# Making the router's gates once for all tiles, and scaling the first expert's results by them

## The chip, the cores and the metric

One core of one Trainium2 chip runs the whole program. The metric is the device time of one execution in microseconds (us); a kernel's time is the median over its runs.

## What is computed

Sliding-window attention gives x (2304 tokens by 512), a mixture of experts with one expert a token turns it into a new x, and a dense layer follows. All is fp32. Cut to what matters here:

```python
logits = xn @ en.T / tau                  # xn, en: rows over their norm
expert_idx = np.argmax(logits, axis=1)
probs = np.exp(logits - logits.max(-1, keepdims=True))
probs /= probs.sum(-1, keepdims=True) + 1e-09
gate_w = probs[np.arange(N), expert_idx]
for e in range(E):                        # E = 8, D = 512, F = 1024
    mask = expert_idx == e
    h = np.maximum(x[mask] @ w1[e], 0.0)
    out[mask] = gate_w[mask, None] * (h @ w2[e])
```

A gate is positive, so it can be multiplied into a token's row ahead of the expert or into the expert's result.

## The kernel before

**Numbers.** TensorE's products take each fp32 operand as a high and a low part (hh and hl, xh and xl, wh and wl) and sum three matmuls. The high part is made by ScalarE (ACT, L87), the low one by VectorE (DVE) or GpSimd (POOL) in L88.

**Attention.** 36 steps, written out as a list; PE's and SyncE's (SP) queues are in the order of the program, those of DVE, ACT and POOL are set by a scheduler. A step makes scores (spb, L241), masked maxima on DVE (L249), exponentials on ACT (pe, L259 and L262), their transposes (pt, L268, copied as pT by ACT in L270), and products with v (po, L280), which DVE scales into xs (L289). Tokens come in 18 tiles of 128. A finished tile is written to x_dram and turned (tpx, L375).

**The router** hangs on the steps. `later(n + d, ...)` puts a piece of it behind a later step, and the table ROUTED gives the distances for the tile groups 0 to 3, 4 to 8, 9 to 12 and 13 to 15; tiles 16 and 17 follow behind the attention. For each group `route_rank` finds the expert of a token as a one-hot row oh (L402 to L410), `route_count` and `route_list` its place in that expert's list, and `part(..., 0, 2)` with `listed` puts the token numbers into the lists: DVE makes Qv (L441), PE sums Qv and lhot into rt (`rt<-Qv,lhot`). Then the gates: `route_norm` (POOL, L450), `route_gate` (twelve small DVE operations and one Exp on ACT, L457 to L473) and `part(..., 2, 5)` with `listed` for the gates' three bf16 parts.

**The first expert.** Behind tile 12 `route_first` chooses the expert with the longest list (efi, L486), and SP loads its weights; ACT makes wh. Its first NA = 208 rows are computed inside the attention's end: `first_rows` gathers them (L108, by POOL's indirect DMAs from the token numbers io), `first_turn` makes their gates go (L492, L493), multiplies the rows (`gated`, L112), transposes them on PE (L119) and splits them into xh and xl. `first_part` is their hidden layer (L132) and second product (pa, L126), evacuated to ya and written to y0_dram.

**Behind the attention** its other 256 rows are gathered in three pieces, the gates of tiles 13 to 17 are made, `route_order` sorts the experts, `route_tokens` gives all lists (idx), and the three pieces are multiplied by their gates and turned. `route_gates` gives all gates by expert (gsl). Then `expert(n)` runs for the eight experts. While one runs, `fetch` gathers the rows of the next and multiplies them by gsl (L112). The buffers of gathered rows, and of expert 0's pieces, are five (pool m3, tag xg); those of `hidden` in PSUM are four (pool p1):

```python
m3 = pool(mc, "m3", 5, side="right", reuse_waits="tile")
p1 = pool(mc, "p1", 4, space=PSUM, reuse_waits="tile")
```

The dense layer follows.

Of the kernel before, what the change touches and what calls it, by code (L numbers as in the profile page):

```python
# [20 lines left out]
def tile_kernel(ctx, tc, q, k, v, emb, tau, w1, w2, w_in, w_out, s_in, b_in, out, x_dram, y_dram, y0_dram, wi_dram, wo_dram):  # L21
# [414 lines left out]

    def part(t0, t1, j0, j1):
        w, ts_ = j1 - j0, slice(t0, t1)
        vb_ = [128, t1 - t0, w, E * KT]
        Qv = rp2.tile(vb_, BF16, tag=f"Qv{w}", name="Qv")  # L440
        made.append(nc.vector.tensor_tensor(Qv, Q[:, ts_].rearrange("p t e k -> p t (e k)").unsqueeze(2).to_broadcast(vb_),  # L441
                                val[:, ts_, j0:j1].unsqueeze(3).to_broadcast(vb_), op=ALU.mult).ins)
        return Qv
# [212 lines left out]
    def fin(slots, pT):  # L656
# [36 lines left out]
        later(n + d[4], lambda: listed(t0, t1, 0, 2, q[0]))  # L693
        if t1 == TL:
            return
        later(n + d[5], lambda: route_norm(t0, t1))
        later(n + d[6], lambda: route_gate(t0, t1), BEHIND)
        later(n + d[7], lambda: q.append(part(t0, t1, 2, 5)), BEHIND)
        later(n + d[8], lambda: listed(t0, t1, 2, 5, q[1]))
        if t1 == TF:  # L700
            later(n + d[9], first_turn)
            later(n + d[4], first_rows)
# [19 lines left out]
    def first_turn():  # L722
        go = first_gates(0, 2)
        for j, r, xg in xga:
            gated(xg, go[:r, j:j + 1])
            turn(ps3, xg, xa, j * 128)
# [26 lines left out]


    def first_part():

        w, ht = sets[0], []
        yield from hidden(ps3, "tp", w, xa, NA, ht, la, NA)
        ya = raw_p.tile([128, 1024], F32, tag="raw", name="ya")[:, :ND * NA].rearrange("p (c n) -> p c n", c=ND)
        for d in range(ND):  # L760
            ps = ps1.tile([128, NA], F32, tag="pt" if d % 2 else "po", name="pa")
            for f in range(NF):
                three(ps, w2part(w, f, d), ht[f], f == 0, f == NF - 1)
            evac(ya, d, ps)
            if d == ND - 1:
                nc.scalar.dma_start(y0cols[:, :, :NA], ya)
            yield
# [3 lines left out]

    ROUTED = {3: ((0, 4), (4, 5, 6, 7, 9, 10, 11, 12, 14)),
# [154 lines left out]
    with tc.manual_schedule(engines={mybir.EngineType.PE}):  # L927
# [8 lines left out]
        for t, xt in xts:  # L936
            route_logits(t, xt)
        route_norm(TF, NTT)
        route_rank(TL, NTT)
# [13 lines left out]
        for j, c0, r, o in ((0, NA - 128, 128, 0), (1, 0, 128, 256 - NA), (2, 0, CAPS[0] - 384, 384 - NA)):  # L953
            xg = m3.tile([128, DM], F32, tag="xg", name="xg")[:r]
            gather(xg, x_dram, io[:r, j:j + 1])
            parts.append((xg, j, c0, r, o))
        route_gate(TF, NTT)
        order = route_order()
        route_tokens(order[1])
        qv = part(TF, NTT, 2, 5)  # L960
        some(7)
        listed(TF, NTT, 2, 5, qv)
        go = first_gates(1, 4)
        some(8)
        for xg, j, c0, r, o in parts:
            gated(xg, go[:r, j:j + 1])
            if j == 2:
                for _ in part_:
                    pass
            turn(ps3, xg, x0, o, c0)  # L970
        route_gates(order[1])
        for _ in part_:
            pass
    xts = {0: x0}

# [9 lines left out]
    def expert(n, w, xt, mid):  # L985
# [10 lines left out]
        for d in range(ND):  # L996
            evac(y, d, ps[d])
        if n == 0:
            nc.scalar.dma_start(y0cols[:, :, NA:NA + N], y)
            nc.scalar.dma_start(ycols[:, :, NA:NA + N], y)  # L1000
# [118 lines left out]
    x2 = []  # L1119
    OV = 4  # L1120
    RR = 1
    for n in range(E):
# [16 lines left out]
        def mid(i):  # L1139
            if n == 0 and i == 0:  # L1140
                begin()
            if last and i == OV:
                fs.close()
# [154 lines left out]
```

## Time and profile before

| | |
|---|---|
| median of 3 runs | 831.58 us (831.35 to 832.79) |
| profiled execution, its own time | 830.12 us |
| its span | 828.4 us |
| mean granted clock of TensorE, as a share of full speed | 0.974 |

The profile is of one execution. Its timelines give each instruction its start and duration in us, with the engine's idle time before it and what ended that in brackets; runs of equal instructions share a row (x4), and matmuls of a row overlap, so that the next row's start tells more than a row's duration. Busy times by stretch end with the granted clock of TensorE (PEclk, 1.00 is 2.4 GHz, 0.50 is 1.2 GHz), the DMA engines' busy share and GB/s. A line number is that of the kernel before.

### The profile page before, as it was taken

How to read it: one execution, taken by the hardware profiler on the slowest of the kernel's cores; microseconds unless marked ns; L12 is line 12 of the kernel's file. 1: busy time of each engine (PE TensorE's matmuls, PEld its weight loads, DVE VectorE, ACT ScalarE, POOL GpSimd, SP SyncE). 2: the span in 40 equal slices, each digit the busy share in tenths (PEclk: the TensorE clock that was granted, in tenths of full speed). 3: DMA queues.
4: the chain of work that ended last, by engine and by line, in shares of the span. 5: the costliest groups of instructions: out<-in, count | busy, mean ns of one | idle time of the engine just before them, and what ended most of it. 6: DMA issues, size and time to landing. Idle time of an engine off the chain costs nothing.

```text
span 828.4 us, 16563 instructions
## 1 busy us (share of the span) xinstructions
PE 783.8 (95%) x6350; PEld 718.3 (87%) x6350; DVE 505.3 (61%) x1310; ACT 394.0 (48%) x796; POOL 195.5 (24%) x184
## 2 busy tenths in 40 slices
PE   6988887889999999899899999999999999999996
PEld 4776676789999999899889999999998999999985
DVE  3766676856778758689575555666646444444442
ACT  6886867415335536445454444444435333332231
POOL 3422335032014244335002222222200110101010
PEclk9997997999999999899999999999999999999999
DMA  9965837156759868775652333333314111100000
GB/s 197 209 182 147 209 97 239 51 185 218 210 178 302 256 223 266 248 244 216 213 186 99 104 102 102 127 127 107 114 63 128 51 52 37 41 26 26 27 26 26
DMA packets 100642, 117.16 MB, mean 141 GB/s; under 512 B 38884, under 2 KB 72164, under 8 KB 100560
## 3 DMA queue, kind: packets, MB, share of 16 engines
q1 hardware_dynamic: 91072, 99.11, 39.7%
q0 software_dynamic: 3232, 10.24, 3.5%
q10 hardware_dynamic: 6256, 6.72, 2.4%
q8 instruction: 51, 0.84, 0.4%
q14 instruction: 31, 0.25, 0.1%
HBM read 91.52 MB, written 24.53 MB: 140 GB/s over the span
## 4 chain that ended last, share of the span: by engine, by line
PE 47%; DMA 2%; issue 1%; DVE 0%; ACT 0%; SPq 0%; POOLq 0%; ACTq 0%
PE p L126 47%; DMA raw<-wi_dram 1%; DMA raw<-wo_dram 1%; DMA y_dram<-y 0%; DMA out_dram<-o,ids 0%; ACT wh L87 0%; DVE wl L88 0%; SPq L96 0%; POOLq L1293 0%; DVE y L747 0%; DVE o L1243 0%; SPq L1112 0%; ACT r L1205 0%; SPq L1039 0%; ACTq L1006 0%
## 5 line engine op out<-in xcount | busy, mean ns | idle before, releaser
L126 PE MATMUL p<-xh,wh 128*128 128x256 f32 x576 | 162.3, 282 | 1.1 <-ACT r L1205 1.1
L126 PE MATMUL p<-xl,wh 128*128 128x256 f32 x576 | 162.4, 282 | 0.0
L126 PE MATMUL p<-xh,wl 128*128 128x256 f32 x576 | 161.7, 281 | 0.0
L1205 ACT ACTIVATE r<-p 128x256 f32<-128x256 f32 x144 | 55.3, 384 | 166.5 <-PE p L126 161.8
L1206 DVE SCALAR_TENSOR_TENSOR r<-r,s_bc 128x256 f32<-128x256 f32 x144 | 79.9, 557 | 77.1 <-ACT r L1205 76.9
L126 PE MATMUL p<-wh,gh 128*128 128x512 f32 x288 | 113.0, 392 | 0.0
L126 PE MATMUL p<-wl,gh 128*128 128x512 f32 x288 | 113.0, 392 | 0.0
L126 PE MATMUL p<-wh,gl 128*128 128x512 f32 x288 | 113.0, 392 | 0.0
L88 DVE TENSOR_TENSOR wl<-raw,wh 128x1024 fp32r<-128x1024 f32 x76 | 107.7, 1424 | 8.2 <-ACT wh L87 8.1
L126 PEld LDWEIGHTS p<-xh,wh 128*128 128x128 f32 x576 | 108.7, 189 | 2.0 <-ACT r L1205 1.3
L126 PEld LDWEIGHTS p<-xl,wh 128*128 128x128 f32 x576 | 108.6, 188 | 0.8
L126 PEld LDWEIGHTS p<-xh,wl 128*128 128x128 f32 x576 | 109.0, 189 | 0.0
L1029 POOL TENSOR_TENSOR fl<-fl,fs 128x512 f32<-128x512 f32 x32 | 45.8, 1433 | 251.2 <-DVE fs L1028 219.2
L87 ACT ACTIVATE wh<-raw 128x1024 fp32r<-128x1024 f32 x80 | 83.3, 1055 | 9.1 <-DMA raw<-in_moe_w_dram 3.9
L126 PE MATMUL p<-hh,wh 128*128 128x256 f32 (+5 forms) x256 | 78.7, 307 | 0.0
L126 PE MATMUL p<-hl,wh 128*128 128x256 f32 (+5 forms) x256 | 76.9, 301 | 0.0
L126 PE MATMUL p<-hh,wl 128*128 128x256 f32 (+5 forms) x256 | 76.9, 300 | 0.0
L1212 ACT ACTIVATE gh<-r,b_bc 128x256 fp32r<-128x256 f32 x144 | 72.5, 503 | 7.7 <-DVE r L1206 7.5
L1213 DVE SCALAR_TENSOR_TENSOR gl<-r,b_bc,gh 128x256 fp32r<-128x256 f32 x144 | 71.2, 494 | 3.1 <-ACT gh L1212 3.1
L1244 POOL DMA_INDIRECT out_dram<-o,ids x18 | 18.6, 1036 | 203.8 <-DVE o L1243 182.8
L126 PEld LDWEIGHTS p<-wh,gl 128*128 128x128 f32 x288 | 54.1, 188 | 12.2
L126 PEld LDWEIGHTS p<-wh,gh 128*128 128x128 f32 x288 | 54.1, 188 | 11.4
(222 smaller groups left out, 1463.9 us busy)
## 6 DMA issues: line engine op xcount, KB each, us to landing
raw<-in_moe_w_dram SPq DMA_DIRECT2D x64, 512.0 KB, 4.9
raw<-y_dram SPq DMA_DIRECT2D x18, 512.0 KB, 3.8
vb<-in_v_dram SPq DMA_DIRECT2D x64, 128.0 KB, 3.7
fr<-in_moe_w_in_dram SPq DMA_DIRECT2D x16, 512.0 KB, 5.2
fr<-in_moe_w_out_dram SPq DMA_DIRECT2D x16, 512.0 KB, 4.0
k<-in_k_dram SPq DMA_DIRECT2D x32, 144.0 KB, 3.3
q<-in_q_dram SPq DMA_DIRECT2D x32, 144.0 KB, 3.3
x_dram<-xs SPq DMA_DIRECT2D x8, 512.0 KB, 3.2
```

Source lines behind the costliest of these rows:

```text
L87: a = nc.scalar.activation(hi, src, AF.Copy)
L88: return a.ins, le.tensor_tensor(lo, src, hi.bitcast(F32), op=ALU.subtract).ins
L126: nc.tensor.matmul(ps, a[x], b[y], start=first and j == 0, stop=last and j == 2)
L1029: nc.gpsimd.tensor_tensor(lf, lf, sg.bitcast(F32), op=ALU.mult)
L1205: nc.scalar.activation(r, ps, AF.Relu)
L1206: nc.vector.scalar_tensor_tensor(r, r, s_bc, r, op0=ALU.mult, op1=ALU.mult)
L1212: nc.scalar.activation(gh, r, AF.Identity, bias=b_bc)
L1213: nc.vector.scalar_tensor_tensor(gl, r, b_bc, gh.bitcast(F32), op0=ALU.add, op1=ALU.subtract)
L1244: nc.gpsimd.indirect_dma_start(out=out, out_offset=bass.IndirectOffsetOnAxis(ap=ids[:, k:k + 1], axis=0), in_=o, in_offset=None)
```

## The change

The gates leave the attention's steps: `route_norm`, `route_gate`, `part(..., 2, 5)` and its `listed` no longer stand in ROUTED. The first expert's rows, the 208 of `first_part` and the 256 others, are turned as they were gathered. The gates of all 18 tiles are made at one place behind the attention: one `route_norm`, one `route_gate` on 18 columns, two Qv of nine tiles each in buffers of m3, and 18 `listed` matmuls together, ahead of expert 0's hidden layer. The first expert's gates go are copied along 128 columns (gob); `first_scale`, behind the second tile of expert 0's hidden layer, turns them by four matmuls (gp) into a row that stands on every partition (grow), and DVE multiplies ya and later expert 0's y by it ahead of their DMAs. `tc.issue_after` keeps the scheduler from putting `route_order`, `route_tokens` and the gates ahead of the last Qv of the token numbers.

```diff
--- before.py
+++ after.py
@@ -434,10 +434,14 @@
         nc.vector.tensor_tensor(Q[:, ts_], oh[:, ts_].unsqueeze(3).to_broadcast([128, n, E, KT]),
                                 kj.unsqueeze(2).to_broadcast([128, n, E, KT]), op=ALU.mult)

-    def part(t0, t1, j0, j1):
+    def part(t0, t1, j0, j1, tp=None):
         w, ts_ = j1 - j0, slice(t0, t1)
         vb_ = [128, t1 - t0, w, E * KT]
-        Qv = rp2.tile(vb_, BF16, tag=f"Qv{w}", name="Qv")
+        n_ = (t1 - t0) * w * E * KT
+        if tp:
+            Qv = tp.tile([128, 1024], BF16, tag="xg", name="Qv")[:, :n_].rearrange("p (t w k) -> p t w k", w=w, k=E * KT)
+        else:
+            Qv = rp2.tile(vb_, BF16, tag=f"Qv{w}", name="Qv")
         made.append(nc.vector.tensor_tensor(Qv, Q[:, ts_].rearrange("p t e k -> p t (e k)").unsqueeze(2).to_broadcast(vb_),
                                 val[:, ts_, j0:j1].unsqueeze(3).to_broadcast(vb_), op=ALU.mult).ins)
         return Qv
@@ -691,14 +695,8 @@
         later(n + d[2], lambda: route_list(t0, t1))
         later(n + d[3], lambda: q.append(part(t0, t1, 0, 2)))
         later(n + d[4], lambda: listed(t0, t1, 0, 2, q[0]))
-        if t1 == TL:
-            return
-        later(n + d[5], lambda: route_norm(t0, t1))
-        later(n + d[6], lambda: route_gate(t0, t1), BEHIND)
-        later(n + d[7], lambda: q.append(part(t0, t1, 2, 5)), BEHIND)
-        later(n + d[8], lambda: listed(t0, t1, 2, 5, q[1]))
         if t1 == TF:
-            later(n + d[9], first_turn)
+            later(n + d[5], first_turn)
             later(n + d[4], first_rows)

     def first_weights():
@@ -720,9 +718,7 @@
             xga.append((j, r, xg))

     def first_turn():
-        go = first_gates(0, 2)
         for j, r, xg in xga:
-            gated(xg, go[:r, j:j + 1])
             turn(ps3, xg, xa, j * 128)

     highs, lows = [], []
@@ -752,26 +748,41 @@
     y0cols = y0_dram.rearrange("(c p) n -> p c n", p=128)


+    early = []
+
+    def first_scale(gob):
+
+        gp = p1.tile([128, KT, 128], F32, tag="tp", name="gp")
+        for j in range(KT):
+            nc.tensor.matmul(gp[:, j], gob[:, j], ident, start=True, stop=True)
+        grow = m1.tile([128, KT * 128], F32, name="grow")
+        nc.scalar.activation(grow, gp.rearrange("p j n -> p (j n)"), AF.Copy)
+        scaled(early[0], grow, 0, NA)
+        nc.scalar.dma_start(y0cols[:, :, :NA], early[0])
+        early.append(grow)
+
+    def scaled(y, grow, c0, n):
+        nc.vector.tensor_tensor(y, y, grow[:, c0:c0 + n].unsqueeze(1).to_broadcast([128, ND, n]), op=ALU.mult)
+
     def first_part():

         w, ht = sets[0], []
         yield from hidden(ps3, "tp", w, xa, NA, ht, la, NA)
         ya = raw_p.tile([128, 1024], F32, tag="raw", name="ya")[:, :ND * NA].rearrange("p (c n) -> p c n", c=ND)
+        early.append(ya)
         for d in range(ND):
             ps = ps1.tile([128, NA], F32, tag="pt" if d % 2 else "po", name="pa")
             for f in range(NF):
                 three(ps, w2part(w, f, d), ht[f], f == 0, f == NF - 1)
             evac(ya, d, ps)
-            if d == ND - 1:
-                nc.scalar.dma_start(y0cols[:, :, :NA], ya)
             yield

     now = [0]
     TOACT = (("k", 0), ("k", 1), ("q", 0))

-    ROUTED = {3: ((0, 4), (4, 5, 6, 7, 9, 10, 11, 12, 14)),
-              4: ((4, 9), (3, 4, 5, 6, 7, 8, 9, 10, 12)),
-              12: ((9, 13), (2, 3, 3, 3, 4, 4, 4, 4, 6, 7)),
+    ROUTED = {3: ((0, 4), (4, 5, 6, 7, 9)),
+              4: ((4, 9), (3, 4, 5, 6, 8)),
+              12: ((9, 13), (2, 3, 3, 3, 4, 6)),
               15: ((13, 16), (2, 3, 3, 3, 4))}
     LATE = 11
     xa = []
@@ -935,7 +946,7 @@
         some(4)
         for t, xt in xts:
             route_logits(t, xt)
-        route_norm(TF, NTT)
+        route_norm(0, NTT)
         route_rank(TL, NTT)
         some(5)
         route_count(TL, NTT)
@@ -954,23 +965,27 @@
             xg = m3.tile([128, DM], F32, tag="xg", name="xg")[:r]
             gather(xg, x_dram, io[:r, j:j + 1])
             parts.append((xg, j, c0, r, o))
-        route_gate(TF, NTT)
-        order = route_order()
-        route_tokens(order[1])
-        qv = part(TF, NTT, 2, 5)
+        with tc.issue_after(made[-1]):
+            order = route_order()
+            route_tokens(order[1])
         some(7)
-        listed(TF, NTT, 2, 5, qv)
-        go = first_gates(1, 4)
         some(8)
         for xg, j, c0, r, o in parts:
-            gated(xg, go[:r, j:j + 1])
             if j == 2:
                 for _ in part_:
                     pass
             turn(ps3, xg, x0, o, c0)
-        route_gates(order[1])
         for _ in part_:
             pass
+        with tc.issue_after(made[-1]):
+            route_gate(0, NTT)
+            qvs = [part(t, t + NTT // 2, 2, 5, tp=m3) for t in (0, NTT // 2)]
+        for t, qv in zip((0, NTT // 2), qvs):
+            listed(t, t + NTT // 2, 2, 5, qv)
+        go = first_gates(0, KT)
+        gob = m3.tile([128, KT, 128], F32, tag="xg", name="gob")
+        nc.vector.tensor_copy(gob, go.unsqueeze(2).to_broadcast([128, KT, 128]))
+        route_gates(order[1])
     xts = {0: x0}

     al.close()
@@ -996,6 +1011,7 @@
         for d in range(ND):
             evac(y, d, ps[d])
         if n == 0:
+            scaled(y, early[1], NA, N)
             nc.scalar.dma_start(y0cols[:, :, NA:NA + N], y)
             nc.scalar.dma_start(ycols[:, :, NA:NA + N], y)
             return
@@ -1118,6 +1134,7 @@
     rest = route_rest(*order)
     x2 = []
     OV = 4
+    GR = 2
     RR = 1
     for n in range(E):
         last = n == E - 1
@@ -1139,6 +1156,8 @@
         def mid(i):
             if n == 0 and i == 0:
                 begin()
+            if n == 0 and i == GR:
+                first_scale(gob)
             if last and i == OV:
                 fs.close()
                 with tc.tile_pool(name="mo", bufs=4) as mo:
```

On DVE, in the router's piece for tiles 9 to 12 inside the attention (L402 to L410 find the expert, L283 to L289 scale a step's result), what goes:

```order
-L461 TENSOR_TENSOR L<-logit,nrm 128x32
 L406 TENSOR_TENSOR eq<-logit,mxs 128x32
 L283 TENSOR_SCALAR rc<-po 128x4
 L408 TENSOR_TENSOR eq<-eq,w_202 128x32
-L463 TENSOR_TENSOR mxs<-mxs,nrm 128x4
 L284 RECIPROCAL rc<-rc 128x4
 L409 TENSOR_REDUCE km<-eq 128x4
-L464 TENSOR_TENSOR L<-L,mxs 128x32
 L289 TENSOR_TENSOR xs<-po,rc 128x2x2x64
 L410 TENSOR_TENSOR oh<-w_202,km 128x32
-L467 TENSOR_REDUCE gt<-L 128x4
```

Three operations of the gates stood between logit and oh and are gone; so are L467 and those behind it.

On PE, the end of expert 0's preparation before (pa is the first part's second product, the xg of 80 columns the last piece of expert 0's rows, tp of 256 columns its hidden layer):

```order
L126 MATMUL pa<-hl,wh 128x208
L126 MATMUL pa<-hh,wl 128x208
L119 MATMUL tp<-ident,xg 128x80 [waits DVE_49]
L119 MATMUL tp<-ident,xg 128x80 x3
L132 MATMUL tp<-xh,wh 128x256 [waits DVE_49,Activation_49]
L132 MATMUL tp<-xh,wh 128x256 x3
L132 MATMUL tp<-xh,wl 128x256 x4
```

The same place in the changed kernel, where this pair of rows for lhot stands 18 times before the hidden layer follows:

```order
L126 MATMUL pa<-hl,wh 128x208
L126 MATMUL pa<-hh,wl 128x208
L119 MATMUL tp<-ident,xg 128x80 [waits DMASW4_49]
L119 MATMUL tp<-ident,xg 128x80 x3
L316 LDWEIGHTS lhot
L316 MATMUL rt<-Qv,lhot 128x96
```

The transposes now wait for the gather's DMA and not for DVE, and the 18 listed matmuls stand where hidden followed at once.

On DVE, the start of expert 0 before (xl are the splits of expert 0's rows, gsl scales the rows of expert 1, hl belongs to expert 0's hidden layer):

```order
L549 TENSOR_REDUCE gsl<-pr 128x32
L112 TENSOR_SCALAR xg<-xg,gsl 128x512
L88 TENSOR_TENSOR xl<-tp,xh 128x4x48
L88 TENSOR_TENSOR xl<-tp,xh 128x4x128
L747 COPY ya<-pa 128x208
L112 TENSOR_SCALAR xg<-xg,gsl 128x512
L88 TENSOR_TENSOR xl<-tp,xh 128x4x80
L112 TENSOR_SCALAR xg<-xg,gsl 128x512
L112 TENSOR_SCALAR xg<-xg,gsl 16x512
L737 SCALAR_TENSOR_TENSOR hl<-tp,hh 128x256
L112 TENSOR_SCALAR xg<-xg,gsl 128x512
```

In the changed kernel, with its own line numbers, behind the splits xl:

```order
L987 COPY gob<-go_3063 128x512
L553 TENSOR_REDUCE gsl<-pr 128x32
L733 SCALAR_TENSOR_TENSOR hl<-tp,hh 128x256
L112 TENSOR_SCALAR xg<-xg,gsl 128x512
L733 SCALAR_TENSOR_TENSOR hl<-tp,hh 128x256
L112 TENSOR_SCALAR xg<-xg,gsl 128x512
L88 TENSOR_TENSOR wl<-raw,wh 128x1024
L733 SCALAR_TENSOR_TENSOR hl<-tp,hh 128x256
L112 TENSOR_SCALAR xg<-xg,gsl 128x512
L88 TENSOR_TENSOR wl<-raw,wh 128x1024
L112 TENSOR_SCALAR xg<-xg,gsl 16x512
L765 TENSOR_TENSOR ya<-ya,grow 128x832
```

The products with gsl stood ahead of the splits and the first hl, and now stand between the hl; gob stands ahead of the first hl and the scaling of ya ahead of the fourth.

## Rows read from the trace of the kernel before

**Rows 1.** Page, part 1: engine, busy us (share of the span), instructions.
```profile
PE 783.8 (95%) x6350; PEld 718.3 (87%) x6350; DVE 505.3 (61%) x1310; ACT 394.0 (48%) x796; POOL 195.5 (24%) x184
```

**Rows 2.** Busy time by stretch: length, engines' busy us, PEclk, DMA share, GB/s.
```profile
118.00:147.20 29.20, 23.92 (x400) 19.53 (x399) 19.83 (x116) 21.80 (x51) 13.90 (x9) 0.82 0.57 192
...
178.80:194.30 15.50, 13.34 (x103) 13.21 (x102) 11.21 (x22) 6.94 (x12) 0.97 (x1) 0.89 0.65 205
```

**Rows 3.** The same view, finer: the three stretches of low granted clock.
```profile
130.40:139.60 9.20, 8.17 (x104) 6.78 (x105) 4.19 (x24) 6.43 (x11) 8.21 (x5) 0.50 0.94 343
...
160.70:164.00 3.30, 3.30 (x19) 3.30 (x17) 3.30 (x11) 0.34 (x1) 0.00 (x0) 0.52 0.00 0
...
181.40:184.80 3.40, 3.40 (x16) 3.40 (x17) 2.36 (x7) 0.38 (x1) 0.00 (x0) 0.52 0.58 195
```

**Rows 4.** Timeline of PE, end of attention: start, us, operation, [idle before, releaser].
```profile
124.16 0.55 PE L375 MATMUL tpx<-ident,xs 128*128 128x128 f32 x3 [0.67 <-DVE xs L289]
...
126.33 0.66 PE L268 MATMUL pt<-ident,pe 128*128 128x128 f32 x4 [0.28 <-ACT pT L270]
127.68 0.66 PE L268 MATMUL pt<-ident,pe 128*128 128x128 f32 x4 [0.69 <-ACT pT L270]
...
130.40 1.03 PE L316 MATMUL rt<-enT,xt 128*64 128x8 f32 x16 [1.47 <-DVE pr L499]
...
143.67 0.95 PE L119 MATMUL tp<-ident,xg 128*128 128x128 f32 x8 [0.69 <-DVE xg L112]
```

**Rows 5.** Timeline of DVE, end of attention.
```profile
120.62 0.17 DVE L457 TENSOR_SCALAR nrm<-nrm 128x4 f32<-128x4 f32 x1 [0.93 <-POOL nrm L450]
...
122.12 0.99 DVE L461 TENSOR_TENSOR L<-logit,nrm 128x32 f32<-128x32 f32 x1
...
127.20 0.13 DVE L486 CAST efi<-ff 1x1 int32<-1x1 f32 x1
...
141.70 1.20 DVE L492 TENSOR_TENSOR go<-li 128x2 f32<-128x2 f32 x1
...
143.13 0.88 DVE L112 TENSOR_SCALAR xg<-xg,go 128x512 f32<-128x512 f32 x2
```

**Rows 6.** Timeline of ACT, end of attention.
```profile
135.73 1.06 ACT L87 ACTIVATE wh<-raw 128x1024 fp32r<-128x1024 f32 x1 [1.28 <-DMA raw<-in_moe_w_dram]
...
144.57 0.40 ACT L262 ACTIVATE pe<-sm,mn 128x128 f32<-128x128 f32 x1 [1.34 <-DVE mn L249]
```

**Rows 7.** Timeline of PE, from the first part to expert 0.
```profile
159.65 0.17 PE L316 MATMUL rt<-oh,tri 128*128 128x16 bf16 x1 [1.90 <-DVE oh L410]
...
172.28 0.39 PE L316 MATMUL rt<-Qv,lhot 128*128 128x96 bf16 x5
172.49 0.34 PE L126 MATMUL pa<-hh,wh 128*128 128x208 f32 x1
...
178.78 0.44 PE L119 MATMUL tp<-ident,xg 80*128 80x80 f32 x4
181.38 1.19 PE L132 MATMUL tp<-xh,wh 128*128 128x256 f32 x4 [2.16 <-DVE xl L88]
...
184.84 0.63 PE L132 MATMUL tp<-xh,wl 128*128 128x256 f32 x4
...
194.26 0.28 PE L126 MATMUL p<-hh,wh 128*128 128x256 f32 x1
```

**Rows 8.** Timeline of DVE, start of expert 0.
```profile
177.13 0.48 DVE L112 TENSOR_SCALAR xg<-xg,go 80x512 f32<-80x512 f32 x1 [1.98 <-DMA xg<-x_dram,io]
...
180.49 0.49 DVE L112 TENSOR_SCALAR xg<-xg,gsl 128x512 f32<-128x512 f32 x1 [2.55 <-DMA xg<-x_dram,idx]
...
188.83 1.22 DVE L88 TENSOR_TENSOR wl<-raw,wh 128x1024 fp32r<-128x1024 f32 x1
```

**Rows 9.** Timeline of POOL.
```profile
154.44 1.20 POOL L450 TENSOR_TENSOR nrm<-ss,half 128x5 f32<-128x5 f32 x1 [11.56 <-DVE ss L380]
```

**Rows 10.** Tile xg from 130 to 215: its gathers, issue to landing.
```profile
DMA to landing us min/median/max: 3.2/5.8/8.5
```

## Prediction

> **What bounds the kernel now.** I read the page's busy shares first, then the busy time by stretch, then the timelines of the stretches that lose something. TensorE (PE) is busy 783.80 of 828.4 us, VectorE (DVE) 505.3 [rows 1]: all that does not fill PE is free as long as PE does not wait for it. By stretch, the losses that this change can reach lie in the end of the attention, 118.00 to 147.20, where PE is busy 23.92 of 29.20 us, and around the start of expert 0, 178.80 to 194.30, with 13.34 of 15.50 [rows 2]. The reader should also see there that busy is not the same as fast: in three stretches the granted clock is 0.50 to 0.52, so the lower of the two levels, 1.2 GHz [rows 3].
>
> The PE timeline of the first place shows the waits: 0.67 for xs of DVE, 0.28 and 0.69 for ACT, 1.47 for DVE's pr, 0.69 for a gathered row tile that DVE multiplies by its gates [rows 4]. Of the second place it shows the last transposes of expert 0's rows at 178.78, a wait of 2.16 us for DVE's xl, hidden from 181.38, and four groups of matmuls at the low clock [rows 7].
>
> **The change, part by part.** The sum is made against the profiled execution, 830.12 us; the median of the runs is 831.58, so 1.46 more, and I add that at the end.
>
> *Attention's end.* Twelve small gate operations a tile group, a Qv of three parts, a pow on POOL and the product of the first rows with their gates leave DVE. Of those that lie ahead of PE's waits, three weigh: DVE waits 0.93 us for POOL's nrm, L461 takes 0.99, go and the product of two tiles 1.20 and 0.88 [rows 5]; with some eight ops of 0.1 us from start to start between them DVE runs up to 2.7 us ahead before the first rows. All five waits of PE [rows 4], 3.80 us together, then lose their cause. What is late next: efi, the number of the first expert, is read at 127.20 [rows 5], and that expert's weights are loaded behind it. ACT rounds them in queue order, waits 1.28 us for one to land, and attention's pe stands behind it; later ACT idles 1.34 us for DVE's mn [rows 6], which go and the products hold up. efi can come 0.67 (xs) plus some 0.9 us of gate operations earlier, 1.6; the wait of 0.69 for the gathered tile and 0.3 of ACT's 1.34 go behind that. Gain 1.6 + 1.0 = 2.6. Bounds: 0, if the weights' landing moves nothing, and 3.8, all the waits. I take 2.6, since the rows name the next releaser. The transposes of the first rows now stand ahead of the last but one step's po and wait for the gather itself; these gathers are issued as much earlier as their list, so I cost that at nothing; if the cover goes, it is case C.
>
> *The wait of 1.90 us for oh* at 159.65 [rows 7]: interleaved gate ops leave DVE. Their successive starts are 0.1 us apart and three stand between logit and oh: 0.3 (0 to 0.4). The low clock behind it [rows 3] I leave as it is.
>
> *Start of expert 0.* Before, from the start of the last transposes to hidden it takes 181.38 - 178.78 = 2.60 us; DVE waits 2.55 us for a gather of expert 1 [rows 8], and the split into xl, which ends PE's wait [rows 7], stands behind that in its queue. After, that product stands behind hidden's first hl, and PE has 18 listed matmuls instead of a pause. Five of them take 0.21 from start to the next start (172.28 to 172.49) [rows 7], so 0.042 each and 0.75 for 18. 0.44 of transposes and 0.75 make 1.2 to 1.25: gain 1.35. Five matmuls leave the block ahead of it: 0.21.
>
> *The clock there.* The first four groups of hidden take 184.84 - 181.38 = 3.46 us, the next 20 take 194.26 - 184.84 = 9.42, 0.47 each [rows 7]. So the low clock [rows 3] costs 3.46 - 1.88 = 1.58. It fell behind the pause of 2.16; without that pause I take it as returned: 1.58 (0 to 1.58).
>
> *What is added.* Four fp32 matmuls gp of 128x128: eight transposes of that size take 0.95 [rows 4], so 0.5. The new copy gob (a pass over 512 elements, 0.4 to 0.6 by the products of 0.88 for two and by the split of 1024 in 1.22 [rows 5, 8]) precedes the first hl on DVE; the scaling of ya passes 832 elements, by the 1.22 of 1024 about 1.0; the last scaling 1.22 lies behind expert 0, in DVE's slack. Hidden's tiles have four buffers, a tile takes 3 x 0.47 = 1.41, so DVE may fall behind by about three of them before PE waits. Expert 1's gathers now wait for PE to free their buffers, and DVE has their products ahead of the later hl. I take 0.4 for all of it; bounds 0 and 2.3, the latter worked out under D.
>
> *The gate chain at the end.* One pow of 18 columns (1.20 for 5 columns [rows 9]: between 1.2 if it is flat and 4.3 if it grows with the columns) ends before DVE needs it, since POOL has nothing else there. Twelve operations of 0.2 to 0.3 on DVE replace as many for 5 tiles; they delay io, the list of expert 0's remaining rows, by 0.65 at most. The last of these rows have landed at 177.13 [rows 8], 1.65 ahead of their transposes at 178.78 [rows 7]: 1.0 stays in hand. The two Qv of 864 elements, by the 1.22 of 1024 again about 1.0 each [rows 8], lie behind io. Cost 0, with case E if that cover is gone.
>
> Sum: -2.6 - 0.3 - 1.35 - 0.21 - 1.58 + 0.5 + 0.4 = -5.1. 830.1 - 5.1 = 825.0; with 1.46, **826.4**.
>
> **The rivals.**
> *B, the clock does not come back.* Hidden's first groups stay slow as they were: 826.4 + 1.6 = 828.0. For it: a low clock also stands in 130.40 to 139.60 [rows 3], where PE is busy most of the time. Against it: the low clock at 181.38 begins right at the pause that goes. The Trainium skill ("TensorE: Matmul & The Clock Gate", section "Why this matters for your kernels") lays a drop in the middle of a kernel to pauses longer than any of these. By that rule the pause of 2.16 us is not the cause and B would hold; the rows show the low clock directly behind pauses of 1.47, 1.90 and 2.16, so they speak against it, and B gets 0.15.
> *C, the attention gives nothing.* If weights, ACT or the first rows' gathers only swap places with the old waits, 2.6 us are lost: 829.0. For it: ACT's wait of 1.28 for a weight [rows 6], and the first rows' transposes, which now stand ahead of po, spb and pt in PE's queue, nearer to their gather. Chance 0.12.
> *E, the gate chain is late.* Single small operations sometimes take about a microsecond (L461 0.99, go 1.20, [rows 5]) where others of their kind take 0.2. Two of those among twelve dependent ones delay io by 0.65 + 1.8; with 1.0 in hand PE waits 1.4 in front of the transposes; a pause of 1.47 has been followed by the low clock [rows 3, 4], 1.6, and up to 1.35 of the transition may go as well: 829.4 to 830.8, say 830.3. Chance 0.12.
> *D, slower: expert 1's gathers block DVE.* Counted from the start of the last transposes, T: the four gathers start behind one another at 1.25 us distance once PE frees the buffers, the fourth at about T + 3.0. With the longest landing seen, 8.5 [rows 10], it is there at T + 11.5, and its product, ya's scaling and hl (together 1.9) end at T + 13.4. PE wants that hl's buffer for its eighth tile at T + 1.25 + 7 x 1.41 + 0.5 = T + 11.6: a wait of 1.8, with the earlier gathers up to 2.3. That alone, with a low clock of 1.6 behind it, is 829.9. Every further microsecond of landing is one of PE: slower than 833.2 from landings of about 12.3, at 13 us 833.9. For it: the gathers share the DMA engines with expert 1's weights. Against: the median landing is 5.8 [rows 10], and then nothing waits. Chance 0.08.
>
> **How the numbers follow.** A, the forecast, 0.53, by itself 823.5 to 828; B 0.15, C 0.12, E 0.12, D 0.08. Down to 823.0 reach the full 3.8 (1.2 more), an uncovered 0.4, and up to 1.8 if the low clock at 130.40 goes too. Up to 830.8 lie B, C and most of E; what is left out is D, the end of E and a little below. A measurement of this kernel can tell about 0.2%, 1.7 us: faster is below 829.9, slower above 833.2. Faster: A, B and most of C, 0.78; same: E and the rest of C, 0.14; slower: D, 0.08.
>
> **What would show it.** In the changed profile PE's waits between 118 and 147 should sum to under 1.5 us and hidden of the first part start at about 144.7; 18 listed matmuls should stand between transposes and hidden with no wait over 0.5, and hidden's first groups take 0.47, not 0.87. B shows as slow groups behind a closed gap, C as waits at the first rows' transposes or at pe, E as a wait at expert 0's transposes or at listed, D as waits of hidden's later groups for hl with DVE idle for an xg gather. If PE's gain behind 194.30 or ahead of 118 is over 0.5 us either way, I have missed a cause there.

## The result, and the profile after

The change takes 821.98 us (median of 6 runs, 817.35 to 825.65), the kernel before beside it 831.47 us (828.41 to 832.84): a ratio of 0.9885, 95% interval 0.9844 to 0.9925. Forecast were 826.4 us and 823.0 to 830.8: the sign was right, the size too small. The profiled execution took 824.65 us (span 822.9 us, mean clock 0.978). Medians below are of all runs of a kernel, while the ratios leave out slow ones, which only `gates_later` has (840.59 and 841.39 of twelve).

Page of the change, part 1, for [rows 1]: PE is busy 3.0 us less, with 8 matmuls more.

```profile
PE 780.8 (95%) x6358; PEld 716.8 (87%) x6358; DVE 500.8 (61%) x1263; ACT 393.1 (48%) x794; POOL 192.9 (23%) x181
```

One pair of traces misleads here, since executions of one kernel differ. I traced both kernels three times and cut PE's timelines at the same instructions; the table has means of three, and in the last column the first traces of both, all in us. The mark "oh of tiles 9 to 12" lies near 124 before, behind the wait of 0.67 for xs [rows 4], so that this part of the forecast for the attention's end stands in that row.

| PE, from one mark to the next | before | change | difference | forecast | first pair |
|---|---|---|---|---|---|
| start to oh of tiles 0 to 3 | 60.83 | 61.55 | +0.7 | 0 | +1.7 |
| to tpx near 79 | 18.87 | 15.94 | -2.9 | 0 | -3.7 |
| to oh of tiles 4 to 8 | 20.91 | 21.53 | +0.6 | 0 | +1.0 |
| to oh of tiles 9 to 12 | 23.14 | 20.66 | -2.5 | -0.67 | -3.8 |
| to hidden of the first part | 22.71 | 22.60 | -0.1 | -1.93 | +2.1 |
| to its pa | 20.31 | 20.18 | -0.1 | -0.3 | +1.7 |
| to expert 0's hidden | 15.36 | 12.95 | -2.4 | -1.56 | -1.9 |
| to its second product | 12.46 | 12.26 | -0.2 | -0.68 | -0.6 |
| to expert 1's hidden | 13.23 | 13.23 | 0 | 0 | 0 |
| expert 1 | 37.75 | 37.01 | -0.7 | 0 | -0.9 |
| experts 2 to 4 | 90.12 | 90.62 | +0.5 | 0 | +0.5 |
| expert 5 to the dense layer | 93.50 | 93.31 | -0.2 | 0 | -0.2 |
| dense layer | 392.15 | 390.78 | -1.4 | 0 | -1.4 |
| sum | 821.3 | 812.6 | -8.7 | -5.1 | -5.4 |

The first pair came out at the forecast sum (824.65 against 825.0), by other terms: that is luck. The two rows of expert 0 up to its second product count together, since before's third trace has its pause ahead of the transposes and not behind them (last section): 27.8 before and 25.2 after, or 27.4 without that trace, so -2.2 where -2.24 was forecast. The +0.7 at the start is a low clock near 46 to 53 that is longer in two of the change's traces; three kernels edited far from there (`go_shared`, `y_late`, `pause_filled`) show it too, so it is not laid to the change. The three readings that matter:

**Ahead of 118, and up to oh of tiles 9 to 12.** Busy time by stretch, before and then the third trace of the change (columns as in [rows 2]): the clock is back.

```profile
60.00:84.00 24.00, 19.41 (x242) 15.23 (x239) 15.52 (x87) 17.49 (x40) 6.25 (x6) 0.79 0.58 153
84.00:118.00 34.00, 29.21 (x500) 23.62 (x500) 24.30 (x136) 25.01 (x56) 10.61 (x10) 0.95 0.68 171
```

```profile
60.00:84.00 24.00, 18.53 (x302) 14.55 (x302) 15.48 (x83) 19.48 (x46) 7.18 (x7) 1.00 0.68 186
84.00:118.00 34.00, 31.32 (x585) 25.43 (x584) 24.65 (x143) 26.76 (x58) 10.85 (x10) 1.00 0.65 161
```

PE's wait there, and DVE ahead of it, in the timelines of the kernel before:

```profile
69.08 1.14 PE L280 MATMUL po<-vb,pT 128*64 128x65 f32 x16 [2.35 <-DVE xs L289]
```

```profile
66.39 0.96 DVE L441 TENSOR_TENSOR Qv<-Q,val 128x256 bf16<-128x256 bf16 x2
67.38 0.16 DVE L283 TENSOR_SCALAR rc<-po 128x4 f32<-128x4 f32 x1
...
68.30 0.17 DVE L284 RECIPROCAL rc<-rc 128x4 f32<-128x4 f32 x1
68.50 0.42 DVE L289 TENSOR_TENSOR xs<-po,rc 128x256 f32<-128x256 f32 x1
```

and in the third trace of the change:

```profile
68.90 0.69 PE L280 MATMUL po<-vb,pT 128*64 128x65 f32 x16 [1.50 <-DVE xs L289]
```

```profile
67.09 0.47 DVE L445 TENSOR_TENSOR Qv<-Q,val 128x256 bf16<-128x256 bf16 x1
67.59 0.16 DVE L283 TENSOR_SCALAR rc<-po 128x4 f32<-128x4 f32 x1
67.79 0.18 DVE L284 RECIPROCAL rc<-rc 128x4 f32<-128x4 f32 x1
...
68.34 0.42 DVE L289 TENSOR_TENSOR xs<-po,rc 128x256 f32<-128x256 f32 x1
```

Before, two Qv and four masked maxima (between the two rc) stand ahead of xs; the scheduler of the changed program puts one Qv and two maxima there. A row gives the shape of its first instruction, so it hides that the second Qv is the gates' own, of three parts. The groups of before's DVE by shape, 55 to 125, have it:

```profile
L441 DVE TENSOR_TENSOR Qv<-Q,val 128x384 bf16<-128x384 bf16 x1 | 0.5, 544 | 0.0
```

From the first Qv to xs it takes 2.11 us before and 1.25 after; 0.49 of the difference goes with the gates' Qv, 0.37 with the two maxima. The wait falls from 2.35 to 1.50 us, and the 16 matmuls behind it take 0.69 and not 1.14: no low clock follows. In all eleven traces with these gates in the steps the wait is 2.35 or 2.36 and the clock of 60 to 84 is 0.79; in all seven without, 1.50 and 0.86 to 1.00. The gain is the clock and not the wait: over the whole stage to tpx PE stands idle 4.1 us before and 4.3, 3.9 and 4.3 after, and is busy 14.6 to 14.9 before and 10.9, 13.4 and 10.9 after.

**118 to 147.** PE of the change, first trace, for [rows 4]:

```profile
122.67 0.66 PE L268 MATMUL pt<-ident,pe 128*128 128x128 f32 x4 [0.88 <-ACT pT L270]
...
124.23 0.64 PE L316 MATMUL rt<-enT,xt 128*64 128x8 f32 x16 [0.28 <-DVE pr L503]
...
129.70 0.69 PE L280 MATMUL po<-vb,pT 128*64 128x65 f32 x16 [1.03 <-DVE xs L289]
...
132.34 1.12 PE L268 MATMUL pt<-ident,pe 128*128 128x128 f32 x4 [1.36 <-ACT pT L270]
...
137.08 0.79 PE L119 MATMUL tp<-ident,xg 80*128 80x80 f32 x4 [1.06 <-ACT xt L377]
...
144.52 1.16 PE L132 MATMUL tp<-xh,wh 128*128 128x208 f32 x4
```

ACT there, for [rows 6]:

```profile
126.25 1.06 ACT L87 ACTIVATE wh<-raw 128x1024 fp32r<-128x1024 f32 x1 [1.81 <-DMA raw<-in_moe_w_dram]
...
130.17 1.06 ACT L87 ACTIVATE wh<-raw 128x1024 fp32r<-128x1024 f32 x1 [1.31 <-DMA raw<-in_moe_w_dram]
```

Of the old waits that for pr is down from 1.47 to 0.28, and those for the gathered tile and the first xs are gone. New ones stand at ACT's pT and xt, 0.88, 1.36 and 1.06, and ACT itself idles for weights, as it did before [rows 6]. The 1.03 for an xs is old: it stood before too, at 136.59, and [rows 4] lacks it. So PE's waits from 118 to 148 sum to 4.9 us, where the forecast had under 1.5 as its sign and before had 5.2. Hidden starts at 144.52, near the forecast 144.7, but because the stages ahead are shorter: luck again.

**Start of expert 0.** PE of the change, first trace, for [rows 7]:

```profile
177.42 0.44 PE L119 MATMUL tp<-ident,xg 80*128 80x80 f32 x4
177.70 0.93 PE L316 MATMUL rt<-Qv,lhot 128*128 128x96 bf16 x18
178.45 0.72 PE L132 MATMUL tp<-xh,wh 128*128 128x256 f32 x4
179.01 0.64 PE L132 MATMUL tp<-xh,wl 128*128 128x256 f32 x4
...
182.77 1.05 PE L757 MATMUL gp<-ident,gob 128*128 128x128 f32 x8
183.58 0.72 PE L132 MATMUL tp<-xh,wh 128*128 128x256 f32 x4
...
190.71 0.28 PE L126 MATMUL p<-hh,wh 128*128 128x256 f32 x1
```

The 18 listed matmuls take 0.75 (177.70 to 178.45), no pause is left, and hidden runs at full clock from its first group (granted clock 1.00 in 178 to 194).

### The profile page after: what moved, and what is told of

Same layout as the page of the kernel before. It is cut to its first block, busy times and chain, and to the rows that moved or that the text cites. A ratio compares the mean times of both kernels' runs of the same rounds, so it can differ in the third digit from the quotient of the medians.

```text
span 822.9 us, 16533 instructions
## 1 busy us (share of the span) xinstructions
PE 780.8 (95%) x6358; PEld 716.8 (87%) x6358; DVE 500.8 (61%) x1263; ACT 393.1 (48%) x794; POOL 192.9 (23%) x181
## 4 chain that ended last, share of the span: by engine, by line
PE 50%; issue 0%; DMA 0%; POOLq 0%; DVE 0%
PE p L126 50%; PE tp L132 1%; DMA out_dram<-o,ids 0%; POOLq L1312 0%; DVE o L1262 0%; POOLq L1263 0%
## 5 line engine op out<-in xcount | busy, mean ns | idle before, releaser
L126 PEld LDWEIGHTS p<-wl,gh 128*128 128x128 f32 x288 | 54.1, 188 | 11.3
```

Of the source, the lines that this page charges most:

```text
L126: nc.tensor.matmul(ps, a[x], b[y], start=first and j == 0, stop=last and j == 2)
```

## The experiments

My theory after the result: the attention ahead of 118 gains by a shorter pause and the clock behind it; expert 0's start gains as forecast; the dense layer gains by where its tiles lie. The rival: executions differ, and one pair of traces shows chance. Ratios below are to the kernel before, run beside each kernel on its chip, with 95% intervals.

### Both kernels again

No edit.

> The kernel before once more, for a second trace. Theory 1: ratio 1.000 within 0.002, and the low-clock stretches of the attention lie elsewhere than in the first trace (20.4 us lost up to 420), while the one behind the pause ahead of expert 0's hidden layer (181 to 185) stands again, since its pause does. Rival (low clock is placed by the program): the same stretches within a microsecond or two.

> The changed kernel once more, for a second trace and more times. Theory 1 (the stretches of low clock move between executions, and every one costs what its length says): the ratio to the kernel before stays near 0.9885, so about 822, and the second trace loses another sum to low clock than the first (16.8 us up to 420) while the stage of hidden of expert 0 still takes full clock from its first group. Rival (the first profile was the typical one and the other runs chance): ratio near 0.993, about 825.

> The kernel before, for a third trace. In three kernels made from it, on one chip, DVE stood for 4.6 us ahead of the copy of ya and the last transposes came 4.4 us later; the two traces of before, on other chips, have no such stop. If it comes from the code of the kernels that were edited, it is absent here; if from the chip, it may stand here or not. The dense layer takes 392.15, expert 1 38.0.

> The changed kernel a third time, for the comparison with the next run on the same chip. Theory: ratio 0.989 to 0.992 to the kernel before; in its trace 390.8 for the dense layer, 37.0 for expert 1, 1.0 to 1.7 from the last transposes to hidden of expert 0, no low clock behind it.

Before: 831.69 us, 0.9991 [0.9965, 1.0017]; its third trace is of one run, 829.67. The change: 825.06, 0.9911 [0.9879, 0.9943], and 819.89, 0.9855 [0.9819, 0.9892]: the first lies between its theory and its rival, the second below what was expected. The expectation that before's low clock would lie elsewhere failed: stretches from 48.2, 68.6, 130.1 and 181.3 stood at 47.8, 68.2, 129.7 and 180.9 the second time, so most of them belong to the program. The stages in which the change is shorter in every trace are that to tpx (15.25, 17.35 and 15.22 against 18.68 to 18.98), that to oh of tiles 9 to 12 (20.66, 20.67, 20.66), expert 0's and the dense layer. From oh of tiles 9 to 12 to hidden the change took 24.83, 21.58 and 21.40: the first trace had a low clock from 131 to 149, the others a shorter one. There the rival holds: that one trace shows chance.

### Gates back in the attention

`gates_early` is the change with the gates of tiles 0 to 12 in the steps again:

```diff
-    ROUTED = {3: ((0, 4), (4, 5, 6, 7, 9)),
+    ROUTED = {3: ((0, 4), (4, 5, 6, 7, 9, 10, 11, 12, 14)),
...
-        route_norm(0, NTT)
+        route_norm(TF, NTT)
...
-            route_gate(0, NTT)
+            route_gate(TF, NTT)
```

> The change with the gates of tiles 0 to 12 left in the attention's steps as before; all else of the change stays (rows not multiplied, results scaled, start of expert 0). Theory 1 (about half of the gain comes from the gate operations leaving the attention, the rest from expert 0's start): 826 to 828. Rival (the gain is nearly all in the rows that are no longer multiplied and in expert 0's start): 821 to 824, as fast as the change. Second rival (it is nearly all in the gates): 829 to 832.

> The change with the gates of tiles 0 to 12 left in the attention, a second time and beside the change. The first pair of traces has the start of the first part, less the time lost to low clock ahead of it, at 132.4 to 132.9 in the change and at 133.6 to 135.8 in the kernels with gates in the attention, so 2.2 us. Theory (this is the attention's share of the gain): this run 2 to 3 us slower than after_third, and 135 again in the trace. Rival (it is scatter of the low clock): the same within 1 us.

825.98 us, 0.9925 [0.9897, 0.9953], and 824.23, 0.9896 [0.9863, 0.993]. Beside the change on the same chip its mean lies 2.1 above (826.6 to 824.5) and 4.7 above (824.4 to 819.7). In both traces the stage to tpx is 18.8 again and that to oh of tiles 9 to 12 is 22.8, hidden of the first part starts at 147.60 and 149.59. So some 2 to 5 us of the gain are the gates' leaving the steps, and the rest is expert 0 and what follows.

`gates03_early` puts back the gates of tiles 0 to 3 alone, far ahead of the place that I had costed:

```diff
+        if t0 == 0:
+            later(n + d[5], lambda: route_norm(t0, t1))
+            later(n + d[6], lambda: route_gate(t0, t1), BEHIND)
+            later(n + d[7], lambda: q.append(part(t0, t1, 2, 5)), BEHIND)
+            later(n + d[8], lambda: listed(t0, t1, 2, 5, q[1]))
```

> The change with the gates of tiles 0 to 3 alone left in the attention at their old distances (10, 11, 12, 14 steps); the other fourteen tiles' gates are made at the end. Theory (these twelve operations hold up xs near 69 us, the pause of 2.35 in place of 1.50 lowers the clock from 68 to 80, 5.1 us): the trace shows PEclk near 0.79 from 60 to 84 and the time is 3 to 5 us above the change, 825 to 827. Rival (the low clock at 68 comes with some executions, whatever stands there): 821 to 823 as the change, and a full clock there.

826.27 us, 0.9903 [0.9871, 0.9934]. Its PE timeline, DVE timeline and busy time by stretch:

```profile
70.48 1.14 PE L280 MATMUL po<-vb,pT 128*64 128x65 f32 x16 [2.35 <-DVE xs L289]
```

```profile
67.79 0.96 DVE L445 TENSOR_TENSOR Qv<-Q,val 128x256 bf16<-128x256 bf16 x2
```

```profile
60.00:84.00 24.00, 19.45 (x257) 15.37 (x256) 16.82 (x93) 16.66 (x37) 6.31 (x7) 0.79 0.57 149
```

The two Qv, the 2.35 and the 0.79 are back, the stage to tpx is 18.73 and that to oh of tiles 9 to 12 22.73. So the gates of these four tiles, without the ones at the attention's end, are enough to bring both stages back; the traces show it, the times alone would not, since the interval overlaps those of the change. No run takes the gates' Qv alone out, or closes this pause alone, so the share of each is read from the order and not tested; and how these gates reach the second stage, some 35 us on, no run shows.

`gates_later` is the kernel before with those gates some six steps later (distances 16, 17, 18, 20).

> The kernel before with the gates of tiles 0 to 3 made six steps later (distances 16, 17, 18, 20), and nothing else. Theory: the pause at 69 us falls to about 1.5, the granted clock of 60 to 84 rises from 0.79 to near 1.00 in the trace, and 2 to 4 us go: 828 to 830 for 832. Rival (the gates then press on a later step, and the low clock falls there): 831 to 833 with a low clock between 85 and 105.

833.88 us, 0.9999 [0.9974, 1.0024]: a miss that tells nothing. The order on DVE is the scheduler's; L461 ran at 56.50 as it had at 56.35, and the wait of 2.35 and the clock of 0.79 stayed.

### The pause at expert 0

`fetch_behind` is the kernel before with expert 1's products behind the first hl on DVE:

```diff
-            gated(xg, gsl[:r, g, j:j + 1])
+            if g == 1:
+                with tc.issue_after(behind_):
+                    gated(xg, gsl[:r, g, j:j + 1])
+            else:
+                gated(xg, gsl[:r, g, j:j + 1])
```

> The kernel before with only one thing moved: the products of expert 1's rows stand behind hl of the first tile of expert 0's hidden layer in VectorE's queue. The step of the prediction on the start of expert 0 says: the pause of 2.16 us shrinks to about 0.5 and the low clock of 1.6 us behind it goes, so 828 to 829 for 831.5. Rival (the clock falls there anyway): 829.5 to 830. Rival (the split is late for another reason): no change.

829.48 us, 0.9973 [0.9947, 0.9999]. Its PE timeline:

```profile
178.80 0.44 PE L119 MATMUL tp<-ident,xg 80*128 80x80 f32 x4
179.77 0.74 PE L132 MATMUL tp<-xh,wh 128*128 128x256 f32 x4 [0.53 <-ACT xh L87]
180.35 0.63 PE L132 MATMUL tp<-xh,wl 128*128 128x256 f32 x4
```

Against [rows 7] the way from transposes to hidden is 0.97 and not 2.60, and hidden to the second product 11.41 and not 12.88, at a clock of 1.00 in 178 to 194 where before had 0.89: 3.1 us in the trace, 2.2 in the times by the ratio. The change's 12.26 against 11.41 is the price of what it adds: 0.85, 0.81 of it the four gp (182.77 to 183.58).

`pause_filled` puts 14 fp32 matmuls into a PSUM tile that nobody reads, between the last transposes and hidden of the kernel before:

```diff
+        for c in range(14):
+            nc.tensor.matmul(spb[:, c % 2, 0, 0], ident, ident, start=True, stop=True)
```

> The kernel before, with 14 matmuls of 128x128 into a PSUM tile that nobody reads, put on PE between the last transposes of expert 0's rows and its hidden layer, where PE waits 2.2 us. Theory (the pause lowers the clock): hidden starts no earlier, but its first four groups take 0.47 and not 0.87 us, so from its start to the second product 11.4 for 12.9 us. Rival (the clock falls there for another reason, as a rule that wants longer pauses would have it): 12.9.

835.41 us, one run: inconclusive. In this execution the pause lay elsewhere (1.8 us ahead of the transposes); the low clock followed it there (178 to 182), and hidden took 11.40. Three traces without the filler (`before_third`, `go_shared`, `y_late`) show the same, so the filler was not put to the test.

### Behind expert 0

`go_shared` is the kernel before with one constant tile for go in place of two, which moves what is allocated behind it:

```diff
-        go = const.tile([128, j1 - j0], F32, name=f"go{j0}")
+        if not go_all:
+            go_all.append(const.tile([128, KT], F32, name="go0"))
+        go = go_all[0][:, j0:j1]
```

> The kernel before, with one tile of 4 columns for the first expert's gates in place of two of 2 and 3 columns, as the change has it; nothing else. In both traces of the change, and with the gates left in the attention, the dense layer (first matmul of 512 columns to the last matmul) takes 390.78 us, in both traces of before and with the fetch moved 392.15, with the same instructions. Theory (the place of the tiles in SBUF, 4 bytes further on, makes the difference): 390.8 here, and 1.4 us in the whole. Rival (it comes from other things of the change, such as code or other pools): 392.15.

832.57 us, 0.9984 [0.9956, 1.0013]: no difference that the times can tell, but its dense layer takes 390.78, as the change's. Costliest groups by shape from 440 to 800, before:

```profile
L126 PE MATMUL p<-xl,wh 128*128 128x256 f32 x514 | 145.0, 282 | 0.0
L126 PE MATMUL p<-xh,wh 128*128 128x256 f32 x514 | 144.7, 282 | 0.0
```

and `go_shared`:

```profile
L126 PE MATMUL p<-xh,wh 128*128 128x256 f32 x512 | 144.1, 281 | 0.0
L126 PE MATMUL p<-xl,wh 128*128 128x256 f32 x512 | 143.7, 281 | 0.0
```

Each matmul is a nanosecond shorter in the mean, without a wait in either. All seven traces with the old two tiles have 392.15 or 392.16, all eleven with one 390.78 or 390.79. Why, no run shows.

`y_late` is the kernel before with the DMAs of expert 0's y behind expert 1's first hh on ACT.

```diff
+            if n == 1 and i == 0:
+                with tc.issue_after(highs[-1]):
+                    late_y.pop()()
```

> The kernel before, with the two DMAs of expert 0's results issued by ACT behind hh of the first tile of expert 1's hidden layer, not ahead of it. In the change the scaling of y puts them there by itself. Theory (the DMAs hold hh up in ACT's queue and are why expert 1 gained 1.0 us): from hidden of expert 1 to hidden of expert 2 it takes 37.0 to 37.3 for 38.0, and the wait for cv (1.0) goes. Rival (that gain came from another order on DVE): 38.0.

832.06 us, 0.9981 [0.9953, 1.0009]. Expert 1 took 36.84 and not 38.0, but the unedited kernel's third trace has 37.10 as well: the cause of expert 1's -0.7 stays open.

### Versions that might beat both

`after_pool` is the change with two of expert 0's weight splits on POOL; `after_defer` is the change with the products of later experts' gathered rows (experts 2 to 7) behind the running expert's second tile on DVE; `after_best` is both; `after_defer3` is `after_defer` for experts 3 to 7 alone:

```diff
-        more = [load_part(src) for src in srcs[ND:]]
+        more = [load_part(src, nc.gpsimd if j < 2 else nc.vector) for j, src in enumerate(srcs[ND:])]
```

```diff
-            gated(xg, gsl[:r, g, j:j + 1])
+            scale_rows.append(lambda xg=xg, r=r, j=j: gated(xg, gsl[:r, g, j:j + 1]))
+            if g < 3:
+                scale_rows.pop()()
...
+            with tc.issue_after(lows[-1]):
+                while scale_rows and i == 1:
+                    scale_rows.pop(0)()
```

> The change, with the low parts of the first two pieces of the first expert's w2 made by POOL and not by DVE. In the change PE still waits 1.7 us for oh, since two of these splits of 1.2 us stand around it on DVE. Theory (the wait is DVE's queue): the wait shrinks to 0.3 to 0.7, the low clock behind it at 159 goes in most executions, so 820 to 822 where the change has 823 to 824 over all its runs. Rival (oh waits for POOL's or PE's work ahead, or the splits come late on POOL and hold the second product): 823 to 826.

> The change with the first two splits of w2 on POOL, and the products of the rows of expert 2 and later ones put behind hl of the second tile of the hidden layer of the expert that runs, where no xl of the next expert waits behind them. On top of after_pool (820.8) theory expects the wait of 1.2 us for xl and most of the 0.7 for cv in expert 1 to go: 819 to 820.5. Rival (the gathers then land in time anyway, and the products only press on hl in the hidden layer): 821 to 823.

> The change with only the products of the rows of expert 2 and later put behind hl of the second tile of the running expert's hidden layer; the splits of w2 stay on DVE. In after_best the stage from hidden of the fifth expert to the dense layer took 87.5 for 92.8 to 93.6 us. Theory (that is the products' place): 88 here too, expert 1 at 37 and not 38.6, so 814 to 817. Rival (it came from w2 on POOL): 93 and 820 to 822.

> The change with the products of the rows of expert 3 and later (not expert 2's) put behind hl of the second tile of the running expert's hidden layer. In after_defer expert 1 took 40.4 us for 37.0, since expert 2's products stood among expert 1's hl, and the last experts 88.6 for 93. Theory: 37.0 and 88 to 89 here, so 815 to 818. Rival (the gain of the last experts hangs on expert 2's products too): 93 and 820 to 822.

820.82 us, 0.9837 [0.9809, 0.9866]; 817.82, 0.9826 [0.9781, 0.987]; 820.32, 0.9843 [0.9811, 0.9874]; **816.11, 0.9815 [0.9771, 0.986]**. The first and the last are as expected, the second is below, and `after_defer` missed its 814 to 817. In `after_pool` the wait of 1.72 for oh is gone and no low clock follows there; one of 1.16 for hl stands 3 us later. PE's waits from 330 to 430, the change (DVEq is DVE's sequencer):

```profile
PE tp L132 <- DVE hl L733: 4.6, 4, 2.3
PE tp L132 <- DVEq L1055: 3.0, 1, 3.0
```

and `after_defer3`:

```profile
PE tp L132 <- DVEq L1059: 2.1, 1, 2.1
PE tp L132 <- DVE hl L733: 1.8, 2, 1.1
```

From expert 5 to the dense layer it takes 88.87 where the change takes 93.31. In `after_defer` the products of expert 2 fall among expert 1's hl, and expert 1 takes 40.43 in place of 37.01; `after_defer3` leaves these where they were (37.73). It has the lowest median and is clearly ahead of before; its interval overlaps those of the other three versions and two of the change's three, so that it beats the change is likely and not shown.

## Why the prediction was right and wrong

*Up to oh of tiles 9 to 12: -0.67 forecast, -4.1 measured. This is the step that failed.* I listed the stretches "that this change can reach" as the end of the attention and expert 0's start, and so never costed the gates of tiles 0 to 8, though they ran on the same DVE queue between the same waits. What they cost was their place: the gates' Qv and the order around it make xs later, PE pauses 2.35 us, and then the clock is low from 68.6 to 78.9. At half speed that would be 5.1 us; the stage is 3.7 shorter without it, and the mean over three traces 2.9. The second piece lies between oh of tiles 4 to 8 and oh of tiles 9 to 12: before, PE waits there 1.28 for an xs near 108, or 1.83, or 2.62 for k from memory, according to the execution, and 0.67 in two of three for the xs of [rows 4]; the change's waits there are 0.83, 0.56 and less, and its stage is 20.66 each time. PE's idle time in it falls from 3.2 to 1.5 in the mean, and in two of before's three traces a low clock stands there (106.2 to 109.6, 110.1 to 113.5), in none of the change's.

*Attention's end: -1.93 of the 2.6 forecast behind that mark, -0.1 measured.* This failed too. The old waits lost their cause as said, but rival C's mechanism came: ACT waited 1.81 and 1.31 for weights, and PE for ACT. PE's idle time in the stage is 4.9 us before and 4.7 after. "efi can come 1.6 earlier" was right in kind: counted from oh of tiles 9 to 12, efi comes 0.85 earlier (1.81 against 2.66; the rest of 121.51 against 127.20 [rows 5] is from the earlier stages), and so do the weights. But they only move the waits. I had named 0 as this term's bound "if the weights' landing moves nothing" and took 2.6. The -0.1 is itself a mean of +2.1, -1.1 and -1.3 by trace: the low clock there, which I had left as it is, takes 16.3 us of the stage in the change's first trace, and 6.8 and 10.2 in the others, against 10.2, 6.8 and 6.8 before. One credit was missing as well: of the 18 listed matmuls I charged to expert 0, I credited the five that left the block ahead of it, and not the 13 that left the attention, 0.5 us at my own 0.042 each.

*The wait for oh:* 1.72 against 1.90 [rows 7], so 0.2; forecast 0.3.

*Start of expert 0: -1.35 and -0.21 forecast.* In the first pair 2.60 became 1.03 and the block ahead 11.93 became 11.65: -1.57 and -0.28, right (the transposes took 0.28 and not 0.44). The 0.75 for 18 listed matmuls was exact.

*The clock there:* 1.58 forecast to return, 1.47 in `fetch_behind`, which does only this; B is refuted. In the six traces with a pause of 1.7 to 2.2 us at hidden or at the transposes ahead of it the low clock stands behind it, also where the pause moved; in the twelve with none over 1.43, `gates_later` among them, there is none. The Trainium skill's "TensorE: Matmul & The Clock Gate", section "Why this matters for your kernels", lays drops in the middle of a kernel to longer pauses; these traces disagree with it for pauses of 2.16 and 2.35 us.

*What is added:* 0.9 forecast, 0.85 measured, and that is luck: four fp32 gp show as eight matmuls and cost 0.81, not 0.5, and the rest, taken at 0.4, next to nothing. Neither D nor E came: from the last transposes to 200 PE shows no wait in the first and third traces and one of 0.45 in the second.

*Behind 194.30:* 0 forecast, -1.8 in the means (-0.7 + 0.5 - 0.2 - 1.4). The prediction said that over 0.5 there, or ahead of 118, would mean a missed cause; there were two, the constant tile and expert 1's start, whose cause is open.

*The median.* I took the changed kernel's profiled execution to lie 1.46 below its median, as before's did; it lay 2.67 above (824.65 to 821.98). This and the missed terms are why 823.0 was too high an end. Mean clock and span of every run give the loss to the low clock as (1 - clock) times span: 21.9 us on the mean of before's 104 runs, 17.2 of the change's 19. By this measure, which counts time in which PE waits as well, 4.7 of the 10.4 us between the means of the runs (832.5 and 822.1) are clock; the rest is fewer waits, work that left, and shorter matmuls.

## What to carry to other kernels

Cost a removed operation at every place where it ran, not only where the profile shows the largest loss: what counts is which wait of the bounding engine it stood ahead of, and whether the clock falls behind that wait. Ask what a row of equal names holds: here the second of two Qv was the operation that the change removes. Trace each kernel more than once before a term of two microseconds is believed; a sum can be right on one pair while its terms are not. When DVE feeds hl to TensorE, work for the next expert belongs behind the hl that is wanted soon, and where the scheduler sets the order, look at the order that came out.

## What the runs showed of the hardware that I had not expected

A pause of 2.35 us at 69 is followed by a clock of 0.5 for some ten microseconds (3.7 us of the stage between the first traces), one of 1.50 at the same place by none or less: a clock of 0.86 (three traces), 0.93 or 1.00 (three) in 60 to 84 against 0.79. One of 1.72 ahead of oh, near 152 to 159, has a low clock beside it in two of the change's traces and none in the other.

The same matmuls of 128x256 take 281 or 282 ns in the mean according to whether go is one constant tile or two (`go_shared`): 1.4 us over the dense layer.

In four traces, one of them the unedited kernel's third, DVE stood still for 4.6 us ahead of the copy of ya; the last transposes came 4.4 us later for it, and the sum from pa to the second product was nearly the same (27.4 without, 28.7 with, and 31.1 in `pause_filled` with its filler). Timeline of DVE in `go_shared`:

```profile
176.92 0.37 DVE L751 COPY ya<-pa 128x208 f32<-128x208 f32 x1 [4.57 <-remote]
```

The releaser tells nothing of the cause; it stays open.
